# Weight rows 128 apart instead of side by side, two gradient tails on all partitions, fewer fills of 8 KB rows

## The chip, the cores and the metric

One core of one Trainium2 chip. The metric is the device time of one execution in microseconds (us). The program runs on one core, so all runs of a timed set are compared with each other and with the kernel before on the same chip; every run timed in rounds is of the fast state (e9 is a single look, whose state is unknown). Ratios of times carry a 95% interval.

## The reference

A decode step with one token: layer norm, attention over the last 4096 of 32768 cached positions (16 query heads, 8 key/value heads, head size 256), a gated block without activation function, and then the gradients of all of it for a given gradient of the output.

```python
W = min(4096, max(256, Sk // 4))                    # 4096 of Sk = 32768
k = repeat(k_cache[:, :, Sk - W:, :], 2)            # v alike
p = softmax(einsum(q, k) * Dh ** -0.5)
h = x + (einsum(p, v) @ wo)                         # q = layernorm(x) @ wq
h2 = h + ((hn @ w_gate) * (hn @ w_up)) @ w_down     # hn = layernorm(h)
# outputs: h2 and the gradients of x, k_cache, v_cache, wq, wo, w_gate, w_up, w_down
```

What matters here: the gradients of the two caches have the full cache size, 2 x 134 MB, and all but the last 4096 positions of each head are zero. These zeros must be written. D is 448 = 3 x 128 + 64, so every weight with 448 rows has three full groups of 128 rows and a rest of 64.

## The kernel before: the parts that matter

The zeros ("fills") are written from a zero region of SBUF, 16 KB per partition, one transfer of 2 MB for each fill (128 rows of 16 KB). The GpSimd queue issues 103 of them, the SyncE queue (SP) the last ones. The upper half of the zero region is borrowed for the second block of gate and up weights; while it is, a fill reads the lower half twice, as rows of 8 KB. These are fills HALF0 to HALF1. The later ones wait until the upper half has been cleared again.

```python
ZW = 8192                                   # elements, 16 KB per partition
HALF0, HALF1 = 42, 63
...
def send_fills(n0, n1, halves=False):
    for reg in fills[n0:n1]:
        if halves:
            ZQ.dma_start(out=reg.rearrange("p (k f) -> p k f", k=2),
                         in_=zeros[:, 0:ZW // 2].unsqueeze(1).to_broadcast([128, 2, ZW // 2]))
        else:
            ZQ.dma_start(out=reg, in_=zeros)
send_fills(0, HALF0)
send_fills(HALF0, HALF1, True)
# ... attention forward, then the gated block in three column blocks n = 0, 1, 2:
            if n == 1:
                nc.vector.memset(ar(ZW // 2, ZW // 2), 0.0)
                send_fills(HALF1, len(fills))
```

Weights with 448 rows are held with three neighbouring rows (3p, 3p+1, 3p+2) on partition p; the 64 rows of the rest lie on 64 partitions (for wq, as halves on 128). The gradients of w_gate and w_up leave the core in the same way:

```python
wq_A = A_wq[0:384, :].rearrange("(p c) j -> p c j", c=3)      # loaded at the start and again for the backward stage
...
for c in range(4):
    kp = DQ if c == 3 else 128                                # DQ = 64
    scale_into(buf[0:kp, c * F:(c + 1) * F], dg_bc[0:kp, i, :], hnT_f[0:kp, c:c + 1])
LD.dma_start(out=ov[0:384, :].rearrange("(p c) f -> p (c f)", c=3), in_=buf[:, 0:3 * F])   # rows of 10752 B
LD.dma_start(out=ov[384:D, :], in_=buf[0:DQ, 3 * F:4 * F])                                 # 64 rows of 3584 B
```

## Time and profile before

| | before |
|---|---|
| median of the first 3 runs | 803.09 us (802.88 to 803.2) |
| span of the profiled execution | 802.6 us |
| moved by the DMA engines | 334.84 MB, 417 GB/s on average |
| busy: PE, DVE, ACT | 57%, 46%, 24% |

From the profile page of the kernel before: the span, the busy shares, the DMA rows of the table of 40 slices of 20 us (busy share in tenths, and GB/s), and the packets of the two large queues (q0 is the GpSimd queue, q1 the SP queue; the columns are packets, MB and share of the 16 engines' span).

```profile
span 802.6 us, 8458 instructions
...
PE 460.6 (57%) x3157; PEld 247.8 (31%) x3180; DVE 368.5 (46%) x1173; ACT 196.1 (24%) x309; POOL 63.6 (8%) x112
...
DMA  9999999999999999999999999999999999999993
GB/s 354 430 430 431 429 428 430 429 429 429 428 424 425 425 419 403 420 423 426 428 421 412 429 430 429 427 428 427 426 425 425 425 425 424 422 408 423 429 438 171
DMA packets 29103, 334.84 MB, mean 417 GB/s; under 512 B 2819, under 2 KB 5638, under 8 KB 6918
...
q0 software_dynamic: 17520, 216.01, 63.7%
q1 hardware_dynamic: 10102, 116.68, 34.7%
...
```

The DMA engines are at 9 tenths from the first slice to the last but one, and no compute engine is near that over the whole span (PE reaches 9 tenths in 14 of the 40 slices, 12 of them from 60 to 300 us). The low first and last slices are the start, and the end, where engines stop one after another.

How the engines stop can be read from the records of the single DMA packets in the trace. They don't name the engine, but the next packet of an engine starts about 4 ns before the last one ends, so in the last 70 us the 16 engines can be told apart. Their ends before, in us, computed this way:

```
784.7 784.9 787.2 787.3 788.3 789.4 789.7 790.9 791.9 793.0 793.4 793.5 793.8 795.3 795.4 801.1
```

None of them has a pause in that stretch. The packet times of the whole run sum to 795.8 us per engine. This counts the overlaps twice, and all of them make some 6 us per engine. What is left, about 789 us, fits engines that begin within the first 2 us and end at 791 on average. So the time is set by the slowest engine's packets, and 801.1 us is within 2 us of the span.

The third reading is the windows of two places where the rate sinks. Columns: window, length, busy us and instructions of PE, PE weight load, DVE, ACT and POOL, granted clock, DMA share, GB/s.

```profile
...
410.00:420.00 10.00, 3.86 (x15) 2.09 (x16) 7.60 (x33) 0.11 (x1) 1.06 (x2) 0.50 1.04 418
420.00:430.00 10.00, 10.00 (x49) 8.87 (x50) 0.00 (x0) 2.09 (x3) 0.53 (x1) 0.79 0.98 387
430.00:440.00 10.00, 10.00 (x62) 9.18 (x62) 0.00 (x0) 2.39 (x4) 0.53 (x1) 1.00 1.03 438
700.00:710.00 10.00, 4.68 (x25) 1.54 (x25) 7.53 (x20) 3.94 (x8) 0.53 (x1) 0.54 1.00 411
710.00:720.00 10.00, 3.52 (x20) 0.74 (x20) 6.48 (x11) 5.93 (x12) 0.00 (x0) 0.50 1.00 407
720.00:730.00 10.00, 0.00 (x0) 0.00 (x0) 0.56 (x1) 0.39 (x1) 0.00 (x0) 0.50 1.02 409
...
```

From 420 to 430 us, where wq is loaded again, the engines are busy but move 387 GB/s (the DMA shares of 1.04, 0.98 and 1.03 show that packets at a window's edge fall to one side, so the three windows should be read together); from 700 to 730 us, where the w_gate and w_up gradients and the last cache gradients leave, about 409.

### The profile page before, as it was taken

What the parts mean: (1) busy time and instruction counts of PE and PEld (TensorE: products, weight loads), DVE (VectorE), ACT (ScalarE), POOL (GpSimd) and SP (SyncE); (2) the same over time, 40 slices, a digit from 0 to 9 for tenths busy, and PEclk for the clock granted to TensorE, in tenths of its full rate; (3) what the DMA queues carried; (4) which work ended last, traced back from release to release, by engine and by line L of the source; (5) the groups of instructions that cost most, each with busy time, mean ns of one, the idle gap of its engine ahead of it and who ended that gap; (6) DMA issues with size and microseconds to landing.
All of it is one profiled execution on the core that took longest, in us unless ns stands there. A gap on an engine that the chain in (4) does not pass through costs nothing.

```text
span 802.6 us, 8458 instructions
## 1 busy us (share of the span) xinstructions
PE 460.6 (57%) x3157; PEld 247.8 (31%) x3180; DVE 368.5 (46%) x1173; ACT 196.1 (24%) x309; POOL 63.6 (8%) x112
## 2 busy tenths in 40 slices
PE   0469999999999992622329397645263054630000
PEld 0334554545645551311219143322122012200000
DVE  2026264463462652255680876766691175860000
ACT  0143314223224000000002045543341034540000
POOL 4000000010100100011110010000000000000000
PEclk9989999999999997555559689776557557655555
DMA  9999999999999999999999999999999999999993
GB/s 354 430 430 431 429 428 430 429 429 429 428 424 425 425 419 403 420 423 426 428 421 412 429 430 429 427 428 427 426 425 425 425 425 424 422 408 423 429 438 171
DMA packets 29103, 334.84 MB, mean 417 GB/s; under 512 B 2819, under 2 KB 5638, under 8 KB 6918
## 3 DMA queue, kind: packets, MB, share of 16 engines
q0 software_dynamic: 17520, 216.01, 63.7%
q1 hardware_dynamic: 10102, 116.68, 34.7%
q10 hardware_dynamic: 1440, 1.61, 0.6%
q8 instruction: 25, 0.41, 0.2%
q14 instruction: 16, 0.13, 0.0%
HBM read 53.69 MB, written 280.59 MB: 416 GB/s over the span
## 4 chain that ended last, share of the span: by engine, by line
PE 35%; DMA 32%; DVE 16%; ACT 4%; issue 2%; another core or an unknown queue 0%; SPq 0%; ACTq 0%; DVEq 0%
DMA out_dram<-arena 17%; PE M_ps L311 10%; PE ok_ps L315 6%; PE rows_ps L255 6%; PE tr_ps L252 4%; DMA dh_bc<-in_grad_out_dram 4%; DMA arena<-in_A_k_cache_dram 4%; DMA arena<-in_A_wo_dram 3%; ACT arena L269 2%; DVE arena L640 2%; DVE arena L641 2%; DVE arena L452 2%; PE dqb_ps L495 2%; DMA arena<-in_B_w_up_dram 2%; DMA arena<-in_B_w_gate_dram 2%
## 5 line engine op out<-in xcount | busy, mean ns | idle before, releaser
L307 DVE TENSOR_SCALAR arena<-arena,p_f 128x256 bf16<-128x256 bf16 x512 | 109.9, 284 | 66.9 <-PE M_ps L311 35.7
L311 PE MATMUL M_ps<-arena 128*128 128x512 bf16 x489 | 120.1, 380 | 1.4 <-issue 0.2
L255 PE MATMUL rows_ps<-arena,vpad 128*16 128x512 bf16 x256 | 86.0, 430 | 23.3 <-DVE arena L603 16.8
L252 PE MATMUL tr_ps<-ident_bf,arena 128*128 128x128 bf16 x1024 | 88.5, 237 | 15.3 <-DMA arena<-in_A_k_cache_dram 9.5
L252 PEld LDWEIGHTS <-arena 128*128 128x128 bf16 x1024 | 66.3, 105 | 65.5 <-issue 54.9
L132 POOL DMA_DIRECT2D out_dram<-arena x82 | 45.1, 550 | 522.2 <-DMA out_dram<-arena 506.3
L269 ACT COPY arena<-tr_ps 128x1024 bf16<-128x1024 bf16 x64 | 61.8, 1015 | 88.6 <-PE tr_ps L252 88.6
L633 PE MATMUL d_ps<-arena,rT 32*128 32x512 bf16 x256 | 44.4, 507 | 63.1 <-DVE arena L641 37.6
L311 PEld LDWEIGHTS <-arena 128*128 128x128 bf16 x512 | 46.2, 99 | 50.8 <-issue 6.5
L315 PE MATMUL ok_ps<-arena 128*16 128x256 bf16 x512 | 57.5, 273 | 0.9 <-DVE arena L296 0.9
L601 ACT COPY arena<-tr_ps 128x1024 bf16<-128x1024 bf16 x32 | 32.5, 1016 | 97.7 <-PE tr_ps L252 40.4
L637 ACT CAST arena<-d_ps 128x512 bf16<-128x512 f32 x64 | 37.6, 587 | 69.5 <-PE d_ps L633 69.5
L640 DVE CAST arena<-d_ps 128x512 bf16<-128x512 f32 x64 | 44.0, 687 | 14.5 <-PE d_ps L633 14.3
L315 PEld LDWEIGHTS <-arena 128*16 128x16 bf16 x512 | 45.4, 90 | 13.9 <-issue 3.4
L641 DVE CAST arena<-d_ps 128x512 bf16<-128x512 f32 x64 | 43.6, 681 | 7.3 <-DMA out_dram<-arena 7.3
L638 ACT CAST arena<-d_ps 128x512 bf16<-128x512 f32 x64 | 38.1, 595 | 6.8 <-DMA out_dram<-arena 6.8
L633 PEld LDWEIGHTS <-rT 32*128 32x128 bf16 x256 | 11.2, 95 | 90.5 <-issue 58.2
L255 PEld LDWEIGHTS <-vpad 128*16 128x16 bf16 x256 | 19.1, 91 | 56.7 <-issue 49.1
L318 ACT COPY arena<-M_ps 128x512 f32<-128x512 f32 x16 | 8.6, 589 | 75.0 <-PE M_ps L311 75.0
L507 DVE CUSTOM_DVE_ANT_0 arena<-arena 128x4096 bf16<-128x4096 bf16 x3 | 13.1, 4423 | 24.3 <-ACT arena L500 24.3
L603 DVE COPY arena<-tr_ps 128x1024 bf16<-128x1024 bf16 x32 | 21.7, 682 | 3.7 <-PE tr_ps L252 3.7
L130 POOL DMA_DIRECT2D out_dram<-arena x21 | 14.0, 666 | 114.3 <-DMA out_dram<-arena 114.3
(196 smaller groups left out, 368.5 us busy)
## 6 DMA issues: line engine op xcount, KB each, us to landing
out_dram<-arena POOLq DMA_DIRECT2D x103, 2048.0 KB, 55.3
out_dram<-arena SPq DMA_DIRECT2D x18, 2048.0 KB, 33.3
arena<-in_A_v_cache_dram SPq DMA_DIRECT2D x10, 2048.0 KB, 49.9
arena<-in_A_k_cache_dram SPq DMA_DIRECT2D x8, 2048.0 KB, 29.4
out_dram<-arena SPq DMA_DIRECT2D x4, 4096.0 KB, 58.8
arena<-in_A_wq_dram SPq DMA_DIRECT2D x2, 3072.0 KB, 14.8
arena<-in_A_wo_dram SPq DMA_DIRECT2D x2, 1792.0 KB, 17.8
out_dram<-arena SPq DMA_DIRECT2D x2, 1792.0 KB, 32.6
```

Of the source, the lines that this page charges most:

```text
L132: ZQ.dma_start(out=reg, in_=zeros)
L252: nc.tensor.transpose(tr_ps[:, dh, i, :], X_sb[:, 4 * q + i, dh * 128:(dh + 1) * 128], ident_bf[:])
L255: nc.tensor.matmul(rows_ps[:], lhsT=pad[:, dh, 16 * q:16 * q + 16], rhs=XT[:, dh].rearrange("p t k -> p (t k)"), start=(q == 0 and dh == 0 ...
L269: sT_ps = dots(kv_at(K_off[g]), KT_slot, vpad[g % 2], rows1, ps_c, "cols", lambda q, XT, ps: nc.scalar.copy(out=XT, in_=ps))
L307: nc.vector.tensor_scalar(out=pK[:, i, hh, :], in0=K_sb[:, t, :], scalar1=p_f[:, 8 * i + c, hh:hh + 1], scalar2=None, op0=ALU.mult)
L311: nc.tensor.matmul(M_ps[:, vh, :], lhsT=V_sb[:, t, vh * 128:(vh + 1) * 128], rhs=pK[:, i, :, :].rearrange("p h d -> p (h d)"), start=(t == ...
L315: nc.tensor.matmul(ok_ps[:, k, :], lhsT=ppad[g % 2][:, 8 * (t % 4) + t // 4, :], rhs=X_sb[:, t, :], start=(g == 0 and k == 0 and t == 0), ...
L633: nc.tensor.matmul(d_ps[:, qi].rearrange("p w d -> p (w d)"), lhsT=rT[32 * q:32 * (q + 1), :], rhs=RB_[32 * q:32 * (q + 1), l, :], start=T ...
L637: nc.scalar.copy(out=stV[:, t:t + 2, :], in_=d_ps[:, :, 0, :])
L638: nc.scalar.copy(out=stK[:, t:t + 2, :], in_=d_ps[:, :, 1, :])
L640: nc.vector.tensor_copy(out=stV[:, t:t + 2, :], in_=d_ps[:, :, 0, :])
L641: nc.vector.tensor_copy(out=stK[:, t:t + 2, :], in_=d_ps[:, :, 1, :])
```

## The change

The intent: with rows c*128 + p on partition p, copies that had to permute columns become plain; the rest of 64 rows goes out from all 128 partitions, as halves of rows; and the clearing of the upper zeros is early enough that only 13 fills instead of 21 need be sent as 8 KB rows.

```diff
-HALF0, HALF1 = 42, 63
+HALF0, HALF1 = 42, 55
...
-    wq_A = A_wq[0:384, :].rearrange("(p c) j -> p c j", c=3)
+    wq_A = A_wq[0:384, :].rearrange("(c p) j -> p c j", c=3)
...            (the same for w_gate and w_up, for the gradient of wq, and for the columns of x)
-        nc.vector.tensor_copy(out=dh_bc[:, 0:384].rearrange("q (p c) -> q p c", c=3), in_=db_ps[:, 0:384].rearrange("q (c p) -> q p c", c=3))
-        nc.vector.tensor_copy(out=dh_bc[:, 384:D], in_=db_ps[:, 384:D])
+        nc.vector.tensor_copy(out=dh_bc[:], in_=db_ps[:])
...            (a small matmul and a scaling for hn_half, rows 384 to 447 of hn on 128 partitions)
+        def outer_half(out, src, col):
+            n = out.shape[1]
+            XB = lnw.tile([128, 2], f32, tag="XB")
+            nc.vector.tensor_scalar(out=XB[:], in0=par_f[:], scalar1=col, scalar2=None, op0=ALU.mult)
+            scale_into(out, src[:, 0:n], XB[:, 0:1])
+            nc.vector.scalar_tensor_tensor(out=out, in0=src[:, n:2 * n], scalar=XB[:, 1:2], in1=out, op0=ALU.mult, op1=ALU.add)
...
-                LD.dma_start(out=ov[0:384, :].rearrange("(p c) f -> p (c f)", c=3), in_=buf[:, 0:3 * F])
-                LD.dma_start(out=ov[384:D, :], in_=buf[0:DQ, 3 * F:4 * F])
+                LD.dma_start(out=ov[0:384, :].rearrange("(c p) f -> p c f", c=3), in_=buf[:, 0:3 * F].rearrange("p (c f) -> p c f", c=3))
+                LD.dma_start(out=ov[384:D, :].rearrange("r (h f) -> (r h) f", h=2), in_=buf[:, 3 * F:7 * F // 2])
```

## The prediction

> **What bounds the kernel.** The 16 DMA engines, from start to end. The slices of the profile page show DMA at 9 tenths in 39 of 40, most at 420 to 430 GB/s; 334.84 MB move in 802.6 us. PE is busy 57%, DVE 46%, ACT 24%. In the trace's DMA packet records, packets of one engine follow each other without gaps; rebuilt from them for the last 70 us, the 16 engines end between 784.7 and 801.1 us, the last one 5.7 us after the one before it. So the time is the packet time of the slowest engine, and compute matters only if it lets the queues run dry. The Trainium skill ("DMA: Bandwidth & Descriptors", "Where 436 GB/s comes from") gives a fabric ceiling of 435 GB/s; the trace's 430 agrees that little is left.
>
> **Costs, from median packet durations in the trace.** 16384 B take 611 ns, 8192 B 309, 24576 B 912, 10752 B 404, 3584 B 140, 1280 B 55. A split costs about 7 ns per added packet. Per engine (sum over packets, divided by 16):
> - 8 fills go from two 8 KB rows to one of 16 KB: 8 x 128 x 7 ns / 16 = -0.45 us.
> - wq, loaded twice, 24 KB rows become three of 8 KB: +0.24 us.
> - dw_gate and dw_up, 10752 B become three of 3584 B: +0.26 us.
> - Their rows 384 to 447: 3584 B on 64 partitions become 1792 B (about 74 ns, an estimate from the durations above) on 128: +0.06 us.
> - dwq, 16 KB become two of 8 KB: +0.06 us.
> Bytes do not change. Sum: about +0.2 us, so nothing. Bursts of slow packets (wq at the start and near 420 us, gate/up gradients near 710 us) cost 1 to 2 us each per engine; other addresses may move them by 1 us either way.
>
> **Compute.** One dh_bc copy instead of two (0.56 + 0.21 us), two small operations more, a second pass over half rows for the gradients. All off the bound: after the last compute, near 720 us, 80 us of transfers remain.
>
> **What would make this wrong.** (1) With HALF1 = 55 the fill queue stops after the 13th half fill (issued at 349.2 us before) until the clearing of the upper zeros ends at 376.8 us: about 23 us. The issue records show 8 fills in flight at most, on average 6.9 after an issue, about 34 us of work at 5 us each; a fast engine has some 25 us. I expect no idle, or a few us on fast engines, which do not set the end. (2) Queues alternate by packet: from 420 to 430 us the 24 KB wq rows held 10.7 engines and the 8 KB fills 5.3 (the skill's "Queues, rings and completion order" says round robin at packet granularity; the trace agrees). After the change wq moves 8 KB against 16 KB fills: the reload takes about 25 us instead of 15, landing near 437 to 443 us, just before DVE reads it at 448.3 us.
>
> **Prediction.** 802.8 us, 800.5 to 805.5 in 8 of 10 cases. Faster by over 2%: 0.01; within 2%: 0.97; slower by over 2%: 0.02.
>
> **What would show it.** DMA stays at 9 tenths in all slices, with 2048 fewer 8 KB packets in the software queue and 1024 more of 16 KB; POOL waits once, about 20 us, for the DVE clearing near 377 us without a dip in GB/s; the wq reload lands later; the span changes by under 3 us. A dip near 380 us would show risk 1, DVE waiting for wq near 448 us risk 2.

## The result, and the profile after

| | before | after |
|---|---|---|
| median, first comparison (4 runs each) | 802.99 us | 802.34 us |
| ratio, first comparison | | 0.9997 (0.9979 to 1.0014) |
| ratio, second comparison (after 5 runs, before 9) | | 0.998 (0.9965 to 0.9995) |
| span of the profiled execution | 802.6 us | 800.5 us |

A ratio here is the mean time of one kernel's runs over that of the other's of the same rounds, so not quite the ratio of the medians. In the second, two of the nine runs of before lie at 805.3 and 805.6 us, above all others of that kernel, and carry part of the difference. The two comparisons together say: the same, perhaps faster by 1 us.

The same lines of the profile page, after:

```profile
span 800.5 us, 8486 instructions
...
PE 459.3 (57%) x3182; PEld 245.9 (31%) x3182; DVE 370.2 (46%) x1176; ACT 196.3 (25%) x309; POOL 62.0 (8%) x112
...
DMA  9999999999999999999999999999999999999994
GB/s 350 431 430 429 428 430 430 427 428 428 431 426 422 428 417 409 420 422 428 433 423 425 424 430 428 429 426 426 424 427 423 426 420 425 423 424 427 423 440 192
DMA packets 29359, 334.84 MB, mean 418 GB/s; under 512 B 2819, under 2 KB 5894, under 8 KB 7814
...
q0 software_dynamic: 16496, 216.01, 63.8%
q1 hardware_dynamic: 11382, 116.68, 34.7%
...
```

The DMA engines are still at 9 tenths everywhere. The software queue has 1024 packets fewer (2048 of 8 KB went, 1024 of 16 KB came), the SP queue 1280 more, and the MB are equal. The ends of the 16 engines after, computed as before:

```
786.0 786.2 787.2 787.6 788.0 788.7 788.9 789.6 789.8 790.3 791.1 791.2 791.3 791.4 795.3 799.0
```

Again one engine ends several us after the others. The packet times sum to 794.7 us per engine, 1.1 us less than before; in a second trace of the kernel after to 795.1.

The windows of the same places, after:

```profile
...
410.00:420.00 10.00, 5.96 (x22) 3.82 (x23) 5.50 (x25) 1.01 (x1) 0.91 (x2) 0.52 1.00 415
420.00:430.00 10.00, 10.00 (x63) 9.20 (x62) 0.00 (x0) 2.35 (x4) 0.90 (x2) 1.00 1.01 422
430.00:440.00 10.00, 10.00 (x63) 9.04 (x62) 0.00 (x0) 1.91 (x5) 0.70 (x2) 1.00 1.01 430
700.00:710.00 10.00, 2.44 (x21) 1.02 (x21) 6.61 (x17) 3.90 (x7) 0.00 (x0) 0.65 1.00 418
710.00:720.00 10.00, 2.96 (x20) 0.44 (x17) 6.45 (x10) 5.37 (x10) 0.00 (x0) 0.50 1.01 424
720.00:730.00 10.00, 0.00 (x0) 0.00 (x0) 0.00 (x0) 0.00 (x0) 0.00 (x0) 0.50 1.00 418
...
```

The three windows of the wq reload now show 415, 422 and 430 GB/s, those near 710 us 418 to 424 instead of 407 to 411. The first three sum to 1267 after and 1243 before, the last three to 1260 and 1227: in both places the bursts of slow packets became smaller. In the packet records, the reload of wq rows took 7.97 us of each engine's time before and 7.43 after; the first load, 9.19 and 9.22.

The stall of the fill queue is there. Two lines of the list of waits of POOL after (waiting engine and line, releaser, us in total, times, longest):

```profile
...
POOL out_dram L132 <- DMA out_dram<-arena: 522.7, 76, 11.8
...
POOL out_dram L132 <- DVE arena L428: 26.3, 1, 26.3
...
```

and the windows around it:

```profile
...
350.00:360.00 10.00, 2.85 (x8) 0.72 (x8) 3.39 (x10) 1.29 (x4) 0.00 (x0) 0.50 1.03 423
360.00:370.00 10.00, 3.69 (x40) 3.19 (x40) 2.78 (x6) 0.00 (x0) 0.00 (x0) 0.50 1.01 422
370.00:380.00 10.00, 3.42 (x19) 1.96 (x20) 8.96 (x22) 1.01 (x1) 2.65 (x5) 0.50 1.02 430
380.00:390.00 10.00, 2.29 (x11) 1.17 (x8) 6.88 (x11) 1.51 (x4) 1.07 (x2) 0.50 1.01 431
...
```

GpSimd waited 26.3 us for the clearing, and the DMA engines noticed nothing. Counting issued fills against landed ones in the records shows why (landed is the mean over engines):

```
issue of fill   us      landed   in flight with this one
54 (last half)  347.7   47.9     7.1
55 (first after the clearing)  374.6   52.9     3.1
59              376.7   53.2     6.8
```

Seven fills in flight were work for the whole stall; 2.1 of them were left when it ended.

### The profile page after: what moved, and what is told of

Same layout as the page of the kernel before. It is cut to its first block, busy times and chain, and to the rows that moved or that the text cites. A ratio compares the mean times of both kernels' runs of the same rounds, so it can differ in the third digit from the quotient of the medians.

```text
span 800.5 us, 8486 instructions
## 1 busy us (share of the span) xinstructions
PE 459.3 (57%) x3182; PEld 245.9 (31%) x3182; DVE 370.2 (46%) x1176; ACT 196.3 (25%) x309; POOL 62.0 (8%) x112
## 4 chain that ended last, share of the span: by engine, by line
PE 35%; DMA 33%; DVE 15%; ACT 4%; issue 2%; another core or an unknown queue 0%; SPq 0%; ACTq 0%; DVEq 0%
DMA out_dram<-arena 19%; PE M_ps L311 11%; PE ok_ps L315 6%; PE rows_ps L255 6%; PE tr_ps L252 4%; DMA dh_bc<-in_grad_out_dram 4%; DMA arena<-in_A_k_cache_dram 4%; ACT arena L269 2%; DMA arena<-in_A_wo_dram 2%; DVE arena L645 2%; DVE arena L454 2%; DVE arena L646 2%; DMA arena<-in_B_w_up_dram 2%; PE dqb_ps L497 2%; DMA arena<-in_B_w_gate_dram 2%; DVE arena L509 2%
## 5 line engine op out<-in xcount | busy, mean ns | idle before, releaser
L311 PE MATMUL M_ps<-arena 128*128 128x512 bf16 x512 | 122.9, 381 | 0.0
L132 POOL DMA_DIRECT2D out_dram<-arena x90 | 48.8, 544 | 560.7 <-DMA out_dram<-arena 522.7
L631 DVE TENSOR_SCALAR arena<-R_sb,tl_f 128x512 bf16<-128x512 bf16 x64 | 17.8, 347 | 2.1 <-ACT R_sb L628 1.9
```

The costliest lines, as they stand in the source:

```text
L311: nc.tensor.matmul(M_ps[:, vh, :], lhsT=V_sb[:, t, vh * 128:(vh + 1) * 128], rhs=pK[:, i, :, :].rearrange("p h d -> p (h d)"), start=(t == ...
```

## The experiments

Three theories were held against each other. Theory 1: the engines' packet time binds; an added packet costs about 7 ns, so each part of the change is worth less than 1 us. Theory 2: the parts are worth several us each and cancel. Theory 3: the chain of compute binds. In the table, "ratio" is to the kernel before on the same chip.

| run | ratio | 95% interval | median us (before) |
|---|---|---|---|
| e1 fills only | 0.9991 | 0.9979 to 1.0004 | 802.83 (803.7) |
| e2 layout only | 1.0006 | 0.9993 to 1.002 | 803.93 (803.7) |
| e3 all fills 8 KB rows | 1.0061 | 1.0048 to 1.0075 | 808.64 (803.7) |
| e4 all fills 4 KB rows | 1.0288 | 1.0273 to 1.0302 | 826.62 (803.7) |
| e5 HALF1 = 48 | 1.016 | 1.0144 to 1.0175 | 817.02 (804.2) |
| e6 HALF1 = 42 | 1.0478 | 1.0461 to 1.0496 | 842.37 (804.2) |
| e7 four fills left out | 0.9737 | 0.9722 to 0.9751 | 782.76 (804.2) |
| e8 more VectorE work | 0.9984 | 0.9969 to 0.9999 | 802.82 (804.2) |
| e9 labelled engines | one look | | 806.9 (802.56) |
| e10 1792 B rows | 0.9982 | 0.9966 to 0.9998 | 802.54 (803.64) |
| e11 uneven last fill | 1.1609 | 1.1591 to 1.1627 | 933.12 (803.64) |
| e12 after, unchanged | 0.998 | 0.9965 to 0.9995 | 802.27 (803.64) |

All gave right results but e7.

### e1 and e2: each part alone

```diff
 e1, in the kernel before:
-HALF0, HALF1 = 42, 63
+HALF0, HALF1 = 42, 55
 e2, in the kernel after:
-HALF0, HALF1 = 42, 55
+HALF0, HALF1 = 42, 63
```

> The kernel before with HALF1 = 55 alone. Theory 1 (packet time of saturated DMA engines; each added packet costs about 7 ns): 8 fills with 1024 fewer packets give -0.45 us, so a ratio to before of 0.999 to 1.000, not to be told from noise. Theory 2 (the parts are large and cancel: fewer 8 KB rows gain, the new layout loses): at least 4 us faster, ratio below 0.995. Theory 3 (the compute chain binds): no change.

> The kernel after with HALF1 back at 63: layout and half rows alone. Theory 1: 1280 added packets x 7 ns / 16, about +0.6 us, less up to 1 us for the calmer bursts near 420 and 710 us: ratio 0.998 to 1.001. Theory 2: at least 4 us slower than before, ratio above 1.005. Theory 3: within 1 us.

Measured: 0.9991 and 1.0006. Both intervals lie inside 0.995 to 1.005, so neither part is worth 4 us, and theory 2 falls. The two point the way that the packet counts do (fewer packets, more packets), but neither differs from 1 by more than its interval, so no sign is claimed.

### e3 and e4: the cost of packets, made large

```diff
-    send_fills(0, HALF0)
+    send_fills(0, HALF0, True)
...
-                send_fills(HALF1, len(fills))
+                send_fills(HALF1, len(fills), True)
```

e4 also makes each such fill four rows of 4 KB from the lower quarter of the zeros (k=4, ZW // 4).

> The kernel after with all 103 fills as two 8 KB rows. Theory 1: 90 x 128 added packets x 7 ns / 16 = +5.0 us, so about 807.4 us, DMA still busy everywhere. Theory 2: the 8 KB rows are what cost, so much more, 15 us or over. Theory 3: no change.

> The kernel after with all fills as four 4 KB rows. The 4096 B packets of the trace take 159 ns, so 16 KB take 636 ns instead of 611 (and 618 for the halves). Theory 1: (90 x 128 x 25 + 13 x 128 x 18) / 16 = +19.9 us, about 822 us (818 to 826). Theory 2: 40 us or over. Theory 3: no change.

Measured: 808.64 and 826.62 us, 0.61% and 2.88% over before. Against the profiled span of after (800.5 us) the spans are 806.6 and 825.0, so +6.1 and +24.5 us for an expected 5.0 and 19.9. Against e2, which ran in the same rounds and differs from e3 only in the rows of 82 fills, e3 is 4.7 us longer (803.93 to 808.64), that is 7.2 ns for each added packet (4.7 us x 16 / (82 x 128)). Theory 1 has the right size for e3, and is short by a fifth for e4 (just over its range of 818 to 826).

But the 7 ns are not made as theory 1 has it. The packet times per engine rise from 794.7 us to 803.5 in e3 and 827.0 in e4, by 8.8 and 32.3 us, more than the spans: the added packets (720 and 2368 per engine) add overlaps too, about 2.5 and 8 us. Without these, 6.3 and 24 us are left, which fits the spans. Of this, packets of median duration make 2.6 and 12 us (5.1 and 20.4 before the overlaps are taken off). The rest is packets slower than their median: their surplus in the two large queues grew from 8.9 us per engine to 12.5 in e3 and 20.7 in e4. Theory 1 left out both the overlaps and the slow packets, and in e3 the two nearly cancel; so the good figure for e3 is partly luck. Why more packets are slow with shorter rows was not tested.

The change turned eight fills of a hundred, so its share of e3's 6.1 us for 90 fills is 0.5 us, too little to be seen.

### e7 and e8: what binds

```diff
 e7:
             fills += [reg[i] for i in range(reg.shape[0])]
+    del fills[-4:]
 e8:
-                for j in range(16):
-                    scale_into(buf[:, j * D:(j + 1) * D], ...)
+                for _ in range(4):
+                    for j in range(16):
+                        scale_into(buf[:, j * D:(j + 1) * D], ...)
```

> The kernel after with the last 4 software fills left out (8.39 MB of zeros not written; the result is wrong on purpose, or right only if the output happened to hold zeros). Theory 1: 4 x 128 x 618 ns / 16 = -19.8 us, about 782.5 us. Theory 3: no change.

> The kernel after with the two wo gradient jobs computed four times each, about 96 more VectorE operations of some 0.24 us, +23 us of DVE in the backward stage. Theory 1: the compute chain ends some 20 us later, still ahead of the backlog of transfers (80 us at its end), so no change, within 1.5 us. Theory 3: up to +23 us, at least +8 us.

Measured: without 8.39 MB of fills 782.76 us, and the profiled span fell from 800.5 to 781.0, 19.5 us for an expected 19.8. With 96 more VectorE operations the time is the same as after (0.9984 and, on another chip, 0.998). The page of e8, its line of busy times, shows that the work was done: DVE 394.3 us, where after has 370.2.

```profile
...
PE 462.5 (58%) x3182; PEld 247.1 (31%) x3182; DVE 394.3 (49%) x1272; ACT 196.6 (25%) x309; POOL 74.8 (9%) x112
...
```

The end of the compute hardly moved either (in e8 the last VectorE work lies between 720 and 730 us, after it ends before 720): the new work mostly went into time that DVE had spent waiting for transfers to release its buffers (the wait of the same line for outgoing transfers fell from 41.6 to 26.2 us). Theory 3 falls: bytes count in full, 24 us of VectorE work not at all.

### e5 and e6: the stall carried too far

```diff
-HALF0, HALF1 = 42, 55
+HALF0, HALF1 = 42, 48          (e6: 42, 42)
```

> The kernel after with HALF1 = 48: the fill queue stops 7 fills earlier, near 297 us, and 8 fills in flight are about 35 us of work plus some 11 us of loads. Theory 1: the DMA engines run dry near 343 us until the clearing (which comes somewhat earlier, near 362 us), so the slices show a dip there and the time rises by about 15 us (8 to 22). Theory 3 (compute chain binds): the loads of the middle stage get the engines to themselves, so no change or a gain of some us.

> The kernel after with HALF1 = 42, no fill of 8 KB rows at all: the change carried to its end. Theory 1: packet cost -0.7 us, but the engines run dry from about 300 us to a clearing near 339 us with only 15 us of loads between, so about +24 us (15 to 32). Theory 2 (8 KB rows are what costs): faster. Theory 3: no change or faster.

Measured: 817.02 us (+1.6%) and 842.37 us (+4.8%). The wait of POOL for the clearing was 67.3 us in e5 and 95.3 us in e6. The DMA rows of the slices, first of e5, then of e6:

```profile
...
DMA  9999999999999999929999999999999999999997
GB/s 351 429 432 428 430 428 430 430 429 424 428 428 421 424 419 406 396 70 392 412 416 428 431 429 426 429 423 425 428 420 429 420 423 425 420 421 432 426 435 331
...
```

```profile
...
DMA  9999999999999991189999999999999999999996
GB/s 357 427 430 429 430 429 429 428 431 425 422 428 426 427 366 55 55 369 412 417 426 432 428 429 427 426 426 422 422 426 429 416 422 419 425 426 427 430 430 266
...
```

e5 has one slice with 70 GB/s, e6 two with 55. The windows of e5 in which the engines were idle:

```profile
...
340.00:350.00 10.00, 2.38 (x29) 2.03 (x29) 6.68 (x14) 0.00 (x0) 0.00 (x0) 0.52 0.68 264
350.00:360.00 10.00, 6.49 (x48) 3.92 (x48) 3.74 (x12) 1.29 (x4) 0.00 (x0) 0.50 0.30 106
360.00:370.00 10.00, 2.03 (x5) 0.57 (x6) 9.48 (x22) 0.04 (x1) 2.98 (x6) 0.50 0.19 79
370.00:380.00 10.00, 3.09 (x20) 2.06 (x19) 7.07 (x13) 2.48 (x5) 2.28 (x5) 0.50 1.03 418
...
```

The DMA share is 0.68, 0.30 and 0.19 in the first three, so 18 us of idle on average; the time rose by 13 us over before, and the span by 15 over that of after, as expected (8 to 22). The difference was given back at the end: the engines, which had spread over 13 us at the end of the kernel after (786.0 to 799.0), ended within 5 us (809.0 to 814.0) in e5, because all of them ran dry and started again together. The fast engines lost more than the slow one. In e6 the share from 310 to 360 us is 0.38, 0.16, 0.18, 0.36 and 0.06, 38.6 us of idle, and the time rose by about 38 us over before (the span by 39.5 over that of after).

For e6 my estimate of 24 us (15 to 32) was too low. I had put the clearing near 339 us, on the ground that the loads before it would run faster alone. GpSimd went on at 358.4 us, only 16 us earlier than after (374.6): between the end of attention and the clearing lies a chain of loads and small operations, which here became only 16 us shorter with the DMA engines nearly free. For the change this means: HALF1 = 55 is on the safe side, and the edge lies between 55 and 48.

### e10: where the issuing queue blocked

In the trace after I had not expected this: the SP queue needed up to 11 us to issue one transfer. The timeline of the SP queue before (start, us, what, number of issues):

```profile
...
701.13 1.69 SPq L643 DMA_DIRECT2D out_dram<-arena  x2
702.87 1.22 SPq L653 DMA_DIRECT2D out_dram<-arena  x1
720.03 2.43 SPq L643 DMA_DIRECT2D out_dram<-arena  x2
722.51 6.81 SPq L653 DMA_DIRECT2D out_dram<-arena  x3
```

and after:

```profile
...
689.99 1.49 SPq L578 DMA_DIRECT2D out_dram<-arena  x1
691.53 8.57 SPq L658 DMA_DIRECT2D out_dram<-arena  x1
700.21 27.27 SPq L648 DMA_DIRECT2D out_dram<-arena  x4
727.68 5.24 SPq L658 DMA_DIRECT2D out_dram<-arena  x1
```

Four issues span 27.27 us after (24.8 of it in the issues themselves, the longest 11.1), where before two span 1.69 and again 2.43. Counted from the records, 71 to 82 packets per engine (mean over engines) were outstanding on this queue when an issue blocked; before, up to 69 with no blocking. Each gradient block of w_gate or w_up is 24 packets per engine after and was 8 before. e10 makes it 48:

```diff
+                for u in range(2):
+                    v = slice(u * F // 2, (u + 1) * F // 2)
-                LD.dma_start(out=ov[0:384, :].rearrange(...), in_=buf[:, 0:3 * F].rearrange(...))
+                    LD.dma_start(out=ov[0:384, v].rearrange(...), in_=buf[:, 0:3 * F].rearrange(...)[:, :, v])
```

> The kernel after with each dw_gate and dw_up block written as two transfers of 1792 B rows: 96 packets per engine instead of 48 for the two blocks together. In the kernel after the issue of the next transfers on the SP queue took up to 11 us each between 691 and 728 us, with about 75 to 80 packets per engine outstanding; before at most 1.8 us with up to 69. If what blocks is a limit on outstanding packets, the blocked time grows (the queue reaches the same 75 to 80 with half the bytes), while the engines stay busy and the time rises by the packet cost alone: 768 packets x 8 ns / 16, about +0.4 us, so 0.998 to 1.002 of before. If the blocking starves the engines, a dip in the slices near 690 to 730 us and over 5 us more. If it is a limit on bytes or transfers, the count at the block doubles.

Measured: the same time as after (0.9982; e12 in the same rounds 0.998). The blocked time grew, to 12.28 + 24.80 + 14.84 us over four issues:

```profile
...
674.11 12.28 SPq L580 DMA_DIRECT2D out_dram<-arena  x1
690.00 24.80 SPq L579 DMA_DIRECT2D out_dram<-arena  x2
714.89 14.84 SPq L580 DMA_DIRECT2D out_dram<-arena  x1
729.78 6.31 SPq L660 DMA_DIRECT2D out_dram<-arena  x1
...
```

The number outstanding when an issue blocked was 74 to 96, neither the same 75 to 80 nor twice that, so what exactly is limited stays open; a limit on the slowest engine's packets would fit, since the engines are not in step, but it was not shown. The blocking did starve the fast engines for a moment (DMA share 0.93 and 375 GB/s from 730 to 740 us), and it cost nothing, since the slowest engine never paused. So the finer rows had a hidden price that this kernel has no occasion to pay: the issue of a transfer behind them is delayed by up to 11 us.

### e9 and e11: which engine ends last, and an attempt to relieve it

e9 sends the last 256 B of each row of the last fill as transfers of 1, 2, ... 15 and 8 rows. The Trainium skill ("DMA: Bandwidth & Descriptors", "Why a DMA increments its semaphore by 16 and not by 1") says that a transfer from this queue over k < 16 engines takes the lowest-numbered k. So the number of small packets names the engine.

```diff
+        LD.dma_start(out=last[:, 0:ZW - 128], in_=ar(ZW, ZW - 128))
+        r0 = 0
+        for k in list(range(1, 16)) + [8]:
+            LD.dma_start(out=last[r0:r0 + k, ZW - 128:ZW], in_=ar(ZW, 128)[0:k])
+            r0 += k
```

> The kernel after; of the last 2 MB fill the last 256 B of each row go out as small transfers of 1, 2, ... 15 and 8 rows at the very end. If a transfer of k rows runs on the k lowest-numbered engines, engine 0 carries 16 packets of 256 B and engine 15 none, so the number of these packets in each rebuilt engine gives its number, and so which engine ends last and by how much. Theory 1: time within 2 us of the kernel after; the ends of the 16 engines again spread over 13 to 17 us. If the last engine is engine 0 or 15, the load can be moved off it with transfers over fewer engines.

Measured: 806.9 us, outside the expected 2 us. Nine of the small transfers were issued only after 799 us, when the rest was done, so the labels stretched the end. But the first six or seven were in the queues in time, and right after the last large packet the rebuilt engines show 1, 3, 4, 5 or more of them, consistent with the rule. The seven engines that carry such packets, 0 to 6 by the rule, ended their large packets between 790.4 and 799.3 us (engine 4 last); the nine without them, 7 to 15, between 784.5 and 792.7.

e11 then deals the last software fill unevenly, to take work off engines 0 to 7:

```diff
-                send_fills(HALF1, len(fills))
+                send_fills(HALF1, len(fills) - 1)
+                reg = fills[-1]
+                ZQ.dma_start(out=reg[0:8], in_=ar(0, ZW)[0:32:4])
+                ZQ.dma_start(out=reg[8:80].rearrange("(i j) f -> i j f", j=9), in_=ar(0, ZW)[64:96:4].unsqueeze(1).to_broadcast([8, 9, ZW]))
+                ZQ.dma_start(out=reg[80:128], in_=ar(0, ZW)[0:48])
```

> The kernel after with the last software fill (128 rows of 16 KB) dealt out unevenly: 48 rows over 16 engines, 72 rows from 8 partitions, and 8 rows from 8 partitions first. In the labelled run engines 0 to 6 ended between 790.4 and 799.3 us and engines 7 to 15 between 784.5 and 792.7. If the second small-engine transfer goes to engines 8 to 15 (round-robin), these get 12 packets of the fill and engines 0 to 7 get 4: the slow half ends 2.4 us earlier, the fast half 2.4 us later, time about -2.4 us (ratio 0.996 to 0.998). If all small transfers go to engines 0 to 7, time about +3 us (1.003 to 1.005). If the time is not set by the slowest engine, no change.

Measured: 933.12 us, for a reason that has nothing to do with balance. Its longest DVE wait:

```profile
...
DVE arena L412 <- DMA out_dram<-arena: 250.3, 1, 250.3
...
```

VectorE stood still for 250 us in the gated block, until outgoing fills were done: it went on at 629.8 us, about when the second of the three new transfers landed (issued at 594.0, 35.7 us to landing). The write that waited touches other bytes than the new transfers read. I take it that reading every fourth partition made the dependency tracking treat these transfers as readers of a much larger part of the buffer; that was not tested. The run tells nothing about balance, and whether evening out the engines gains the few us between the last engine and the mean stays open.

### e12: the kernel after once more

> The kernel after, unchanged, on the same chip as the balance run and timed in more rounds: ratio to before 0.999 to 1.000, and again one or two engines that end 3 to 6 us after the others.

Measured: 0.998 (0.9965 to 0.9995), slightly under the expected 0.999. Engines end at 785.6 to 790.9 (twelve of them), 794.3, 795.6, 795.8 and 799.1 us: one engine again 3 us behind the next. No run beat both kernels with a right result by more than the noise.

## Why the prediction was right

It said 802.8 us, the same, and 802.34 was measured (802.27 in the second comparison).

- **The bound.** Right, and now shown by e7 and e8: 8.39 MB less is 19.5 us less, 24 us of VectorE work more is nothing.
- **The packet costs.** Right in sum, but the 7 ns per added packet were mis-sized: with the overlap of 3.5 ns taken off, an added packet of median duration costs about 3.5 ns, and the slow packets, which come on top (e3, e4), were not in the sum. For the 256 packets that the change adds this is 0.06 us. The estimated 74 ns for 1792 B was 74 in the trace. The sum of medians per engine rose by 0.06 us (783.77 to 783.83, in the three queues that carry the program's data), predicted +0.2. Single terms differ: the 912 ns for rows of 24 KB were the median of the reload alone, over both loads it was 921, which makes +0.10 of the +0.24 for wq; splitting the 10752 B rows cost 0.03 us instead of 0.26 (6.72 to 6.76 us per engine), because before some of those packets were slower than the median that I used, and the halves on 128 partitions gave 1.19 us for 1.34.
- **The bursts.** Predicted to move by 1 us either way; they fell. In the two large queues the time over the median packets went from 10.1 to 8.9 us per engine (9.3 in e12), mainly near 710 us (by 1.0) and less at the wq reload. This is the 1 us that the change may have gained, and it comes from calmer packets. The kept traces tell which part calmed those near 710 us: from 700 to 730 us the surplus is 1.4 us in before and 1.7 in e1 (fills only), but 0.4 in e2 (layout only), after, e8, e10 and e12. So it was the layout, not the smaller number of 8 KB rows. It is no sure gain: from 440 to 640 us the surplus was 1.7 us before and 2.0 to 2.6 in the other six, and e2 as a whole was no faster than before. Whether the other row lengths or the other addresses calm the packets, and why, no run shows.
- **The stall of the fill queue.** Predicted 20 to 23 us, without a dip: 26.3 us, and no dip. e5 and e6 show that the mechanism is real and what it costs when HALF1 goes too low.
- **Queues that alternate by packet.** The prediction cited the skill ("Queues, rings and completion order"). The reload of wq by 8 KB packets against 16 KB fills was to last about 25 us and land near 437 to 443 us: the 384 rows landed at 436.9 us, 26.3 us after their issue (16.6 before), the rest at 443.4. From 420 to 430 us the SP queue held 5.7 engines and the fills 10.3; packets of 309 and 611 ns in turn would give 5.4 and 10.6. One figure was misread: DVE started on wq at 443.9 us before, not at 448.3, which was the second of three operations. After, it started at 440.5, 3.6 us after the landing, and it was released by the scaled dq from ACT, as before. It was closer than the text had it.
- **Compute.** Off the bound, as predicted, and not smaller: the one dh_bc copy takes 0.63 us where two took 0.56 + 0.21, but three passes over half rows take 4.6 us where one took 2.3, and VectorE is busy 370.2 us instead of 368.5.
- **What it missed.** The blocking of the SP queue by transfers of 24 packets per engine. It did no harm here.

So the expected gain of "fewer 8 KB rows" was never large: 0.5 us of 800. The bytes are the same, the engines were already full, and what the new layout saves VectorE in copies, or adds in half rows, lies beside the bound.

## What to carry to other kernels

If the DMA engines are busy from end to end, cost a layout change in packets: count those that appear and vanish, take their durations from the trace less the overlap with the next packet, and divide by 16. Expect slow packets on top, so check the sum with one run that makes the change large: here halving rows of 16 KB cost 7 to 8.5 ns for each added packet by the clock, of which 3.5 came from median durations, so only changes of ten thousand packets or of megabytes are seen. A queue that keeps the engines fed may stop for as long as the work in flight lasts (here 26 us with 7 fills of 2 MB in flight) at no cost, and beyond that the idle time is paid, here 13 to 15 of 18 us and 38 to 40 of 39, so measure the depth in flight before moving a wait. The end is set by the slowest engine, so short pauses of the others are free.

## What the Trainium skill lacked or had wrong

- "DMA: Bandwidth & Descriptors", "Why small descriptors are slow (HBM only)", gives a fixed overhead of about 3 cycles per packet and calls it a matter of small descriptors. With the fabric's 850 MHz of the same page that is an estimate of 3.5 ns. The trace agrees: two packets of 8192 B took 2 x 309 ns and one of 16384 B 611 ns, so 7 ns more, of which 3.5 ns is overlap. What the page lacks is the slow packets that come with shorter rows (3.6 of the 6.1 us of e3), and that rows as long as 4 KB still cost 3% in a kernel bound by transfers (e4).
- The same page, "Latency and other measured facts", calls DMA engines 7 and 15 usually slower than the others. In the one labelled run, engines 7 to 15 ended at 784.5 to 792.7 us and 0 to 6 at 790.4 to 799.3, if the page's own rule of the lowest-numbered k holds; so neither 7 nor 15 was among the last five.
- No page has the blocking of the SP queue: with about 70 to 96 packets per engine outstanding, a single issue took up to 11 us (19 us in e10) instead of about 0.3 us.
- "Where 436 GB/s comes from" and "Queues, rings and completion order" agree with this case in the fabric ceiling and the round robin: 430 GB/s in steady stretches, with single slices up to 440 (a packet counts where it starts), and while rows of 24 KB (and after them some of 4 KB) met 8 KB rows in two queues, they held 10.7 and 5.3 engines. But where the first of the two says that for transfers between HBM and SBUF the HBM side binds at about 358 GB/s, this program of one core kept 430.
